# A decay table laid out with its heads innermost and moved on ScalarE's DMA queue

## The chip, the cores and the metric

The kernel runs on one core of a Trainium2 chip. The metric is the device time of one execution in microseconds, smaller is better. TensorE does matmuls, VectorE and ScalarE elementwise work (ScalarE also moves data out of PSUM), GpSimd slow elementwise work and scattered DMAs; in this kernel every ordinary DMA is issued from SyncE's queue.

## The reference

Three layers follow each other: a decayed linear attention (2 batches, 8 heads, 768 positions, head size 64), an MLP with a hard-swish, and a mixture of 8 experts in which each expert takes at most 192 of the 1536 tokens, in the order of their logits.

```python
# attention, per block: Dmask[i,j] = lam**(i-j) for i >= j, else 0
intra = (qb @ kb.T * Dmask) @ vb
inter = (qb * lam_pow) @ kv_state
kv_state = lam_block * kv_state + (kb * rev_pow).T @ vb
...
h = x @ w_in                     # 1536 x 512 @ 512 x 2048
g = h * clip(h + 3, 0, 6) / 6
x2 = g @ w_out                   # 2048 x 512
...
logits = x2 @ w_gate             # greedy assignment, capacity 192
out[mask] = relu(x2[mask] @ w1[e]) @ w2[e]
```

## The kernel before, in words

The 1536 tokens are 12 chunks (c0 to c11) of 128, six for each batch. For a chunk, attention needs its raw data (`raw`, loaded in two halves: q and k for the scores, then v and k), the products of scores and decay mask (`sm`), the keys scaled by decay (`kd`, eight ScalarE steps, one a head), the running state (`sbd`, faded on ScalarE and added to on VectorE), and then `outs` on TensorE (`xo`). The result goes out of PSUM as two f16 parts (`xT`: high part on ScalarE, L504, rest on VectorE, L505).

The MLP's first product (`h`, L221 to L223, three matmuls for each pair of f16 parts) needs `xT` and converted weights. w_in and w_out come as 64-bit floats, in 8 blocks each, and `weights` turns a block into two f16 parts: clear the sign (L381 on VectorE or L383 on ScalarE), a max (L385, VectorE or GpSimd), shift (L387), two merges (L389, L391), then the high part on ScalarE (L406) and the low one on VectorE (L416). After a product, ScalarE and VectorE make g (L535, L536, L406, L416). Then come the logits (L610), seven rounds of token assignment (L800 to L809 on VectorE) with the second product (`x2p`, L647) run beside them, scattering, and the experts (L922, L952).

The order of the work is written by a planner: `add` records a step with an engine, an estimated cost, dependencies, buffers and a key; `run` repeatedly emits the step that by its estimates can start first, with the lower key first among those that start within a small window. The order it writes is fixed in each engine's queue, so an engine waits at a step even if a later one could go. Every load on SyncE is such a step.

All decays come from one small table, `tab`. Each partition holds the powers of four heads (128 zeros, 1, then 128 powers), which VectorE makes by seven doublings (`powers`, L268 to L277). Two DMAs on SyncE's queue write the rows of two partitions to DRAM (`tz`, L306), and a third (L311) reads them back into all partitions with a start that is one element later in each, so that every partition gets its row of the decay mask for 8 heads: 1024 pieces of 512 bytes. These DMAs stand between the loads of the first chunk and the others. `kdec` (L359) and `sm` (L458) wait for the third; `qd` (L443) and the fade (L474) use the powers themselves.

Of the kernel before, what the change touches and what calls it, by code (L numbers as in the profile page):

```python
# [5 lines left out]
F32 = mybir.dt.float32  # L6
# [3 lines left out]
AF = mybir.ActivationFunctionType  # L10
# [38 lines left out]
class Plan:  # L49
# [143 lines left out]
def fused_kernel(ctx, tc, raw_d, lam_d, win_d, wout_d, wg_d, w1_d, w2_d, out):  # L193
# [23 lines left out]
    def C(shape, dt, name):  # L217
        return cst.tile(shape, dt, name=name)
# [4 lines left out]
        te.matmul(ps, ll, rh, start=False, stop=stop)  # L223


    lam = C([P, 4], F32, "lam")
    sy.dma_start(lam, lam_d)
    raws = {}
    plan.clk["ve"] = 0.6
# [31 lines left out]
    tabb = buf("B", [P, 2052], F32, "tab")  # L261
    sbdb = buf("B", [P, 3, 4, 64], F32, "sbd")
    held += [tabb, sbdb]
    for b in held[2:]:
        b.left += 1
    pw, dec = (lambda: tabb.tile[:, 0:1028].rearrange("p (h x) -> p h x", h=4)), None

    def powers():  # L268
        x = pw()
        ve.memset(x[:, :, 0:128], 0.0)  # L270
        ve.memset(x[:, :, 128:129], 1.0)
        ve.tensor_copy(x[:, :, 129], lam)
# [26 lines left out]
    pw = pw()
    tab = tabb.tile  # L300
    sbd = [sbdb.tile[:, i] for i in range(3)]
    dec = tab[:, 1028:2052].rearrange("p (r h i) -> p r h i", r=2, h=4)
    qdec = pw[:, :, 129:257]
# [3 lines left out]
    plan.dma = max(plan.dma, 6.7)
    plan.clk["sp"] = 5.4
    plan.steps = list(parts[1])
    plan.run()  # L310
# [43 lines left out]
    plan.clk.update(ve=5.4, ge=3.4, se=2.0, sp=7.6)  # L354
# [71 lines left out]
    def attention(c, key):  # L426
# [7 lines left out]
        if s < 5:  # L434
            kd = buf("Q", [P, 512], F32, f"kd{c}")

            def kdm():
                for h in range(8):
                    se.activation(kd[:, 64 * h:64 * h + 64], r[:, 3, 64 * h:64 * h + 64], AF.Copy, scale=kdec[:, h:h + 1])  # L439
            t_kd = add("se", 1.6, kdm, ld + [t_kdec], [r, kd], key)  # L440
        if s:
            qd = buf("Q", [P, 4, P], F32, f"qd{c}")
            t_qd.append(add("ve", 0.62, lambda: ve.tensor_tensor(qd[:], r[:, 0].rearrange("p (h i) -> p h i", h=4), qdec, op=OP.mult),  # L443
                            ld[:1], [r, qd, tabb], key))
# [10 lines left out]
        for i in range(2):  # L455
            sm = buf("Q", [P, 4, P], F32, f"sm{c}_{i}")
            sms.append(sm)
            t_mk.append(add("ve", c_ve(512), lambda i=i, sm=sm: ve.tensor_tensor(sm[:], pss[i][:], dec[:, i], op=OP.mult),  # L458
                            [t_ss, dec_in], [pss[i], sm, tabb], key))
        if s < 5:  # L460
            pk = buf("pE" if c > 3 else "pC", [P, 4, 64], F32, f"kv{c}")

            def kv():
                for hp in range(4):
                    for par in range(2):
                        cl = slice(P * hp + 64 * (par ^ hp & 1), P * hp + 64 * (par ^ hp & 1) + 64)
                        te.matmul(pk[64 * par:64 * par + 64, hp], kd[:, cl], r[:, 2, cl], start=True, stop=True)
            t_kv = kv_done[c] = add("pe", 0.66, kv, [t_kd] + ld, [kd, r, pk], key)
# [532 lines left out]
def pack(inputs):  # L1001
# [17 lines left out]
    lam = np.repeat(lam, 64, axis=0)  # L1019
# [22 lines left out]
```

## Time and profile before

| | |
|---|---|
| median of 3 runs | 514.68 us (512.02 to 515.46) |
| profiled execution | 515.91 us, of which span 514.0 us |
| TensorE / VectorE / ScalarE / GpSimd busy | 485.0 / 397.8 / 309.0 / 166.6 us |
| DMA | 77.86 MB, mean 151 GB/s |
| mean granted TensorE clock | 0.986 |

Busy times add up every stage; the kernel has a start, a long MLP stage to about 205 us, the assignment to about 340 us and the experts, each with its own limit. Matmuls overlap in the records, so a busy TensorE can still have room.

### The profile page before, as it was taken

What the parts mean: (1) busy time and instruction counts of PE and PEld (TensorE: products, weight loads), DVE (VectorE), ACT (ScalarE), POOL (GpSimd) and SP (SyncE); (2) the same over time, 40 slices, a digit from 0 to 9 for tenths busy, and PEclk for the clock granted to TensorE, in tenths of its full rate; (3) what the DMA queues carried; (4) which work ended last, traced back from release to release, by engine and by line L of the source; (5) the groups of instructions that cost most, each with busy time, mean ns of one, the idle gap of its engine ahead of it and who ended that gap; (6) DMA issues with size and microseconds to landing.
All of it is one profiled execution on the core that took longest, in us unless ns stands there. A gap on an engine that the chain in (4) does not pass through costs nothing.

```text
span 514.0 us, 10307 instructions
## 1 busy us (share of the span) xinstructions
PE 485.0 (94%) x4241; PEld 296.7 (58%) x4243; DVE 397.8 (77%) x707; ACT 309.0 (60%) x486; POOL 166.6 (32%) x174
## 2 busy tenths in 40 slices
PE   7687998999999999999999999999969999999995
PEld 3476444688785444534434443556459676776762
DVE  7689999988688877589899889877524878889620
ACT  1476959764556664377669558745423767687510
POOL 2013343120222220167347436618860312223211
PEclk9889999999999999999999999999979999999999
DMA  7999326220264550000000000667368999995011
GB/s 224 400 416 412 148 83 246 84 42 2 83 246 91 97 94 8 2 1 1 1 1 2 1 1 7 240 246 240 132 149 261 327 400 356 360 354 215 1 42 41
DMA packets 44910, 77.86 MB, mean 151 GB/s; under 512 B 33080, under 2 KB 34112, under 8 KB 38720
## 3 DMA queue, kind: packets, MB, share of 16 engines
q1 hardware_dynamic: 42752, 70.82, 41.0%
q0 software_dynamic: 2112, 6.39, 3.3%
q8 instruction: 33, 0.54, 0.4%
q14 instruction: 13, 0.11, 0.1%
HBM read 63.46 MB, written 6.40 MB: 136 GB/s over the span
## 4 chain that ended last, share of the span: by engine, by line
DVE 38%; issue 22%; PE 18%; POOL 8%; ACT 8%; DMA 5%; POOLq 0%; SPq 0%; DVEq 0%; ACTq 0%
PE x2p L647 9%; DVE G L809 7%; DVE r L536 4%; DVE G L800 3%; DVE g L416 3%; POOL w L410 3%; POOL out L877 2%; ACT kd L439 2%; DVE sm L458 2%; ACT g L406 2%; DVE eq L782 2%; PE h L221 2%; DVE wid L391 2%; PE cp L828 2%; PE h L223 2%
## 5 line engine op out<-in xcount | busy, mean ns | idle before, releaser
L647 PE MATMUL x2p<-wo,g 128*128 128x512 f16 (+1 forms) x576 | 124.6, 362 | 0.0
L221 PE MATMUL h<-xT,wi 128*128 128x256 f16 (+2 forms) x304 | 90.8, 306 | 2.8 <-DVE r L536 2.8
L222 PE MATMUL h<-xT,wi 128*128 128x256 f16 (+2 forms) x304 | 90.7, 306 | 0.0
L223 PE MATMUL h<-xT,wi 128*128 128x256 f16 (+2 forms) x304 | 90.6, 306 | 0.0
L647 PEld LDWEIGHTS <-g 128*128 128x128 f16 x576 | 52.5, 99 | 55.6 <-issue 10.5
L775 POOL TENSOR_SCALAR eq<-mrow,m 128x128 bf16<-128x128 f32 x56 | 56.7, 1030 | 84.6 <-DVE on L748 52.1
L416 DVE SCALAR_TENSOR_TENSOR w<-ws,w 128x1024 f16<-128x1024 f32 x58 | 71.4, 1276 | 5.8 <-ACT w L406 5.8
L922 PE MATMUL hp<-xs,w 128*128 128x192 f16 x768 | 67.4, 251 | 3.8 <-DMA xs<-xsa 3.8
L922 PEld LDWEIGHTS <-w 128*128 128x128 f16 x768 | 65.1, 100 | 7.6 <-issue 5.2
L952 PE MATMUL po<-w,h 128*64 128x512 f16 (+1 forms) x384 | 64.1, 380 | 0.1
L406 ACT ACTIVATE w<-ws 128x1024 f16<-128x1024 f32 x64 | 63.9, 1048 | 0.1
L809 DVE TENSOR_SCALAR G<-mrow,m 128x1408 bf16<-128x1408 f32 (+10 forms) x77 | 52.0, 706 | 0.0
L385 POOL TENSOR_SCALAR wod<-wod 128x1024 f32<-128x1024 f32 x8 | 22.5, 2818 | 89.3 <-ACT wod L383 75.5
L406 ACT ACTIVATE g<-r 128x512 f16<-128x512 f32 (+1 forms) x52 | 30.8, 595 | 30.5 <-DVE r L536 29.6
L952 PEld LDWEIGHTS <-h 128*64 128x64 f16 (+1 forms) x384 | 29.0, 104 | 31.8 <-issue 1.7
L416 DVE SCALAR_TENSOR_TENSOR g<-r,g 128x512 f16<-128x512 f32 (+1 forms) x52 | 34.3, 662 | 11.4 <-ACT g L406 11.0
L536 DVE SCALAR_TENSOR_TENSOR r<-r,h 128x512 f32<-128x512 f32 (+1 forms) x52 | 33.1, 639 | 10.1 <-ACT r L535 9.8
L535 ACT ACTIVATE r<-h,c 128x512 f32<-128x512 f32 (+1 forms) x52 | 33.4, 644 | 10.9 <-PE h L223 10.8
L803 ACT ACTIVATE G<-mrow,m 128x1536 bf16<-128x1536 f32 (+3 forms) x28 | 39.4, 1407 | 0.8
L222 PEld LDWEIGHTS <-wi 128*128 128x128 f16 x304 | 30.6, 101 | 15.9 <-issue 3.2
L928 ACT ACTIVATE rr<-hp 128x384 f32<-128x384 f32 x32 | 15.6, 490 | 40.0 <-PE hp L922 39.8
L221 PEld LDWEIGHTS <-wi 128*128 128x128 f16 x304 | 30.5, 100 | 15.0 <-issue 1.5
(154 smaller groups left out, 693.2 us busy)
## 6 DMA issues: line engine op xcount, KB each, us to landing
ws<-w SPq DMA_DIRECT2D x32, 1024.0 KB, 9.3
raw<-raw SPq DMA_DIRECT2D x24, 512.0 KB, 10.0
wis<-w_in SPq DMA_DIRECT2D x8, 1024.0 KB, 14.1
wos<-w_out SPq DMA_DIRECT2D x8, 1024.0 KB, 7.8
tab<-tz SPq DMA_DIRECT2D x1, 512.0 KB, 6.3
wt<-wo SPq DMA_TRANSPOSE x16, 3.2
xsa<-xa,pos POOLq DMA_INDIRECT x12, 4.9
xsb<-xb,pos POOLq DMA_INDIRECT x12, 2.7
```

Source lines behind the costliest of these rows:

```text
L221: te.matmul(ps, lh, rh, start=start, stop=False)
L222: te.matmul(ps, lh, rl, start=False, stop=False)
L223: te.matmul(ps, ll, rh, start=False, stop=stop)
L406: h = add("se", c_se(n), lambda: se.activation(dst()[0], src(), AF.Copy, scale=sc), deps, bufs, key, reserve)
L416: lo = add("ve", c_ve(n), lambda: ve.scalar_tensor_tensor(dst()[1], src(), sc, dst()[0], op0=OP.mult, op1=OP.subtract), [h], bufs, key)
L536: t = add("ve", c_ve(nf * T), lambda: ve.scalar_tensor_tensor(r[:], r[:], 6.0 * 2.0 ** -11, ps[:], op0=OP.min, op1=OP.mult), [t], [ps, r], ...
L647: te.matmul(ps[:], gsl(y, fc, j), w[:, z, fc % 4, d0:d1], start=(fc + y + z == 0), stop=(fc == 15 and y == 1))
L775: t_eq.append(add("ge", 1.06, lambda i=i, eq=eqs[0], mrow=mrow: ge.tensor_scalar(eq[:, i], mrow[:, P * i:P * i + P], m[:, i:i + 1], None, ...
L803: se.activation(G[:, z, 0:o], mrow[:, 0:o], AF.Sign, scale=-1.0, bias=m[:, i:i + 1])
L809: ve.tensor_scalar(G[:, z, o:], mrow[:, o:], m[:, i:i + 1], None, op0=OP.is_le)
L922: te.matmul(ps[:, i], w[:, z, kk % 2, cl], x[:, 2 * kk + y, CAP * i0:CAP * i0 + CAP], start=(i + kk + y + z == 0), stop=(i == 1 and kk == ...
L952: te.matmul(o, h1[e][:, y, k, cl], w2[e, fh][0][:, zz, f], start=(k + y + zz == 0), stop=(k == 7 and y == 1))
```

## The change

- **Table.** `xp` holds, in every partition, the powers of all 8 heads with the head as the innermost index (256 x 8). One DMA of 8 KB on ScalarE's queue writes one partition of it to DRAM, a second one on the same queue reads it back with a start 8 elements later in each partition: 128 pieces of 4 KB. ScalarE then turns the order from (position, head) into (head, position) (`dec_in`, one step of 1024 columns), and makes the powers of the own heads (`own`, two steps of 512 columns on 64 partitions) for `qd` and the fade. SyncE's queue holds loads alone, in the order w0, q0, q1, v0, v1.
- **kd.** The eight scalings of a chunk become two planner steps of four, with a key that is 2 higher, so that `xT` of the same chunk goes ahead of them.
- **Conversion.** Blocks 1 and 2 of w_in clear the sign on ScalarE (L383) and take the max on GpSimd (L385), as blocks 3 to 7 do; block 0 stays on VectorE.

```diff
-    lam = C([P, 4], F32, "lam")
+    lam = C([P, 8], F32, "lam")
...
+    xpb = buf("B", [P, 256, 8], F32, "xp")
+    tabb = buf("B", [P, 512 + 1024], F32, "tab")
+    sbdb = buf("B", [P, 768 + 1024], F32, "sbd")
...
     def powers():
-        x = pw()
-        ve.memset(x[:, :, 0:128], 0.0)
-        ve.memset(x[:, :, 128:129], 1.0)
-        ve.tensor_copy(x[:, :, 129], lam)
+        x = xpb
+        ve.memset(x[:, 0:127], 0.0)
+        ve.memset(x[:, 127:128], 1.0)
+        ve.tensor_copy(x[:, 128], lam)
         n = 1
         while n < 128:
-            ve.tensor_tensor(x[:, :, 129 + n:129 + 2 * n], x[:, :, 129:129 + n],
-                             x[:, :, 128 + n:129 + n].to_broadcast([P, 4, n]), op=OP.mult)
+            ve.tensor_tensor(x[:, 128 + n:128 + 2 * n], x[:, 128:128 + n],
+                             x[:, 127 + n:128 + n].to_broadcast([P, n, 8]), op=OP.mult)
             n *= 2
...
-    tz = dram.tile([2, 4, 256], F32, name="tz")
-    for par in range(2):
-        sy.dma_start(tz[par:par + 1], pw[64 * par:64 * par + 1, :, 0:256])
...
-    sy.dma_start(dec, bass.AP(tensor=tz.tensor, offset=tz.offset + 1, ap=[[1, P], [256, 8], [1, P]]))
...
+    tz = dram.tile([256 * 8], F32, name="tz")
+    se.dma_start(tz[:].rearrange("(o n) -> o n", o=1), xpb.tile[0:1].rearrange("p n c -> p (n c)"))
+    se.dma_start(decs, bass.AP(tensor=tz.tensor, offset=tz.offset, ap=[[8, P], [1, 1024]]))
...
+    dec_dma = Step({}, [], [], 0, 0, 0)
+    dec_dma.end, dec_dma.on = 9.6, "dma"
...
+    def own():
+        for par in range(2):
+            pr = slice(64 * par, 64 * par + 64)
+            se.activation(qdec[pr], xpb[pr, 128:256, 4 * par:4 * par + 4].rearrange("p i h -> p h i"), AF.Copy)
+    t_own = add("se", 1.2, own, (), [xpb, tabb], 1)
+    dec_in = add("se", 1.1, lambda: se.activation(dec.rearrange("p r h i -> p (r h) i"), decs.rearrange("p (i c) -> p c i", c=8), AF.Copy),
+                 [dec_dma], [tabb, sbdb, xpb], -1)
...
-            early = by_cols and k < 3
+            early = by_cols and k < 1
...
-            def kdm():
-                for h in range(8):
+            def kdm(z):
+                for h in range(4 * z, 4 * z + 4):
                     se.activation(kd[:, 64 * h:64 * h + 64], r[:, 3, 64 * h:64 * h + 64], AF.Copy, scale=kdec[:, h:h + 1])
-            t_kd = add("se", 1.6, kdm, ld + [t_kdec], [r, kd], key)
+            t_kd = [add("se", 0.96, lambda z=z: kdm(z), ld + [t_kdec], [r, kd], key + 2) for z in range(2)]
...
-                        se.activation(sb[:, hp], old[:, hp], AF.Copy, scale=pw[:, hp, 256:257])
+                        se.activation(sb[:, hp], old[:, hp], AF.Copy, scale=qdec[:, hp, 127:128])
```

## Rows read from the trace of the kernel before

**Rows 1.** Busy time by stretch: engines, TensorE's granted clock, DMA share, GB/s

```profile
0.00:20.00 20.00, 12.58 (x81) 6.21 (x82) 13.37 (x35) 6.41 (x19) 2.65 (x18) 1.00 0.83 281
20.00:40.00 20.00, 17.13 (x256) 14.74 (x256) 16.78 (x28) 13.59 (x46) 2.81 (x1) 0.83 1.02 415
60.00:80.00 20.00, 19.05 (x142) 9.49 (x140) 19.86 (x28) 13.61 (x32) 5.83 (x2) 1.00 0.24 82
80.00:100.00 20.00, 18.67 (x176) 11.20 (x176) 19.97 (x34) 16.07 (x42) 5.91 (x2) 1.00 0.49 183
...
98.00:355.00 257.00, 253.64 (x2166) 141.15 (x2164) 215.43 (x439) 160.89 (x211) 90.93 (x83) 1.00 0.22 64
```

**Rows 2.** The chain that ended last, pieces in order: start us, us, what

```profile
6.01 1.72 DMA tz<-tab
8.25 7.60 DMA raw<-raw
15.93 3.93 ACT kd L439 x16
...
28.15 1.91 ACT kd L439 x8
...
345.17 9.77 PE x2p L647 x60
```

**Rows 3.** Timeline, 0 to 31 us: start us, us, engine, line, operation [idle before <-releaser]

```profile
2.48 0.85 DVE L272 COPY tab<-lam 128x4 f32<-128x4 f32 x1 [0.61 <-DMA lam<-lam]
...
7.81 0.39 SPq L311 DMA_DIRECT2D tab<-tz  x1
...
14.12 0.38 DVE L359 COPY kdec<-tab 128x2 f32<-128x2 f32 x4 [2.51 <-DMA tab<-tz]
14.40 2.48 DVE L458 TENSOR_TENSOR sm<-S,tab 128x512 f32<-128x512 f32 x4
...
15.98 1.09 PE L498 MATMUL xo<-sm,raw 128*64 128x128 f32 x16 [2.45 <-DMA raw<-raw]
...
19.77 0.63 ACT L504 ACTIVATE xT<-xo 128x256 f16<-128x256 f32 x2
20.16 0.75 DVE L505 SCALAR_TENSOR_TENSOR xT<-xo,xT 128x256 f16<-128x256 f32 x2 [2.15 <-ACT xT L504]
...
21.98 0.29 PE L221 MATMUL h<-xT,wi 128*128 128x128 f16 x1
...
25.79 0.45 PE L494 MATMUL xo<-qd,sbd 64*64 64x128 f32 x8
...
30.36 0.76 DVE L505 SCALAR_TENSOR_TENSOR xT<-xo,xT 128x256 f16<-128x256 f32 x2 [1.12 <-ACT xT L504]
```

**Rows 4.** The instructions on tile tab: ns min/median/max, first and last start us

```profile
L275 DVE TENSOR_TENSOR tab<-tab x7: 166/191/424, 3.4 to 4.8; 128x4 f32<-128x4 f32 x1, 128x8 f32<-128x8 f32 x1, 128x16 f32<-128x16 f32 x1, 128x32 f32<-128x32 f32 x1
```

**Rows 5.** Busy time by stretch of 1 us; the last two columns are DMA share and GB/s

```profile
10.00:11.00 1.00, 0.90 (x16) 0.90 (x16) 1.00 (x2) 0.00 (x0) 0.00 (x0) 1.00 1.03 207
...
16.00:17.00 1.00, 1.00 (x16) 0.83 (x16) 1.00 (x3) 1.00 (x5) 0.00 (x0) 1.00 1.00 414
```

**Rows 6.** GpSimd's output scatters (L877): in 400 to 445 us, then 445 to 514 us

```profile
DMA to landing us min/median/max: 6.1/8.1/8.3
...
DMA to landing us min/median/max: 2.7/2.7/8.2
```

**Rows 7.** The instructions on tile wid: ns min/median/max, first and last start us

```profile
L387 DVE TENSOR_SCALAR wid<-wid x8: 678/684/1400, 7.8 to 77.0; 128x1024 int32<-128x1024 int32 x8
...
L383 ACT ACTIVATE wid<-wis x5: 1140/1151/1160, 35.3 to 67.7; 128x1024 f32<-128x1024 f32 x5
L385 POOL TENSOR_SCALAR wid<-wid x5: 2766/3067/3492, 36.5 to 68.9; 128x1024 f32<-128x1024 f32 x5
L381 DVE TENSOR_SCALAR wid<-wis x3: 682/684/699, 6.4 to 35.9; 128x1024 int32<-128x1024 int32 x3
L385 DVE TENSOR_SCALAR wid<-wid x3: 677/681/695, 7.1 to 37.8; 128x1024 f32<-128x1024 f32 x3
```

More of the change, by code (lines that the diff above doesn't have):

```diff
@@ L259, in load_w @@
             deps, [st], key, 3, 1 << 20)
-    tabb = buf("B", [P, 2052], F32, "tab")
-    sbdb = buf("B", [P, 3, 4, 64], F32, "sbd")
-    held += [tabb, sbdb]
+    xpb = buf("B", [P, 256, 8], F32, "xp")
+    tabb = buf("B", [P, 512 + 1024], F32, "tab")
+    sbdb = buf("B", [P, 768 + 1024], F32, "sbd")
+    held += [tabb, sbdb, xpb]
     for b in held[2:]:
         b.left += 1
-    pw, dec = (lambda: tabb.tile[:, 0:1028].rearrange("p (h x) -> p h x", h=4)), None
     def powers():
-        x = pw()
-        ve.memset(x[:, :, 0:128], 0.0)
-        ve.memset(x[:, :, 128:129], 1.0)
-        ve.tensor_copy(x[:, :, 129], lam)
+        x = xpb
+        ve.memset(x[:, 0:127], 0.0)
+        ve.memset(x[:, 127:128], 1.0)
+        ve.tensor_copy(x[:, 128], lam)
         n = 1
         while n < 128:
-            ve.tensor_tensor(x[:, :, 129 + n:129 + 2 * n], x[:, :, 129:129 + n],
-                             x[:, :, 128 + n:129 + n].to_broadcast([P, 4, n]), op=OP.mult)
+            ve.tensor_tensor(x[:, 128 + n:128 + 2 * n], x[:, 128:128 + n],
+                             x[:, 127 + n:128 + n].to_broadcast([P, n, 8]), op=OP.mult)
             n *= 2
-    FIRST = [["w0", "q0"], ["q1"], ["v0", "v1"]]
     ld_raw, win_ld, first = {}, {}, {}
-    for i, nm in enumerate(sum(FIRST, [])):
+    for i, nm in enumerate(["w0", "q0", "q1", "v0", "v1"]):
         c = int(nm[1])
@@ L288, in fused_kernel @@
             first["q%d" % c], first["v%d" % c] = ld_raw[c]
-    for i, nm in enumerate(sum(FIRST, [])):
+    for i, nm in enumerate(["w0", "q0", "q1", "v0", "v1"]):
         first[nm].key, first[nm].reserve = i - 9, 0
-    add("ve", 3.9, powers, (), [tabb])
-    add("ge", 0.1, lambda: ge.memset(sbdb[:, 0], 0.0), (), [sbdb])
+    add("ve", 4.4, powers, (), [xpb])
+    add("ge", 0.1, lambda: ge.memset(sbdb[:, 0:256], 0.0), (), [sbdb])
+    add("ge", 0.1, lambda: ge.memset(tabb[:, 0:1], 0.0), (), [tabb])
     held += [raws[c] for c in ld_raw] + [x[0] for x in win_ld.values()]
-    for b in held[4:]:
+    for b in held[5:]:
         b.left += 1
-    parts = [[first[n] for n in p] for p in FIRST]
-    plan.steps = [x for x in plan.steps if x not in parts[1] + parts[2]]
     plan.run()
[L299 to L303, printed above, removed]
-    tz = dram.tile([2, 4, 256], F32, name="tz")
-    for par in range(2):
-        sy.dma_start(tz[par:par + 1], pw[64 * par:64 * par + 1, :, 0:256])
[L307 to L310, printed above, removed]
-    sy.dma_start(dec, bass.AP(tensor=tz.tensor, offset=tz.offset + 1, ap=[[1, P], [256, 8], [1, P]]))
-    plan.dma = max(plan.dma, 8.8) + 1.46
-    plan.steps = parts[2] + [late_warm]
+    qdec = tabb.tile[:, 0:512].rearrange("p (h i) -> p h i", h=4)
+    decs = tabb.tile[:, 512:1536]
+    sbd = [sbdb.tile[:, 256 * i:256 * i + 256].rearrange("p (h d) -> p h d", h=4) for i in range(3)]
+    dec = sbdb.tile[:, 768:1792].rearrange("p (r h i) -> p r h i", r=2, h=4)
+    tz = dram.tile([256 * 8], F32, name="tz")
+    se.dma_start(tz[:].rearrange("(o n) -> o n", o=1), xpb.tile[0:1].rearrange("p n c -> p (n c)"))
+    se.dma_start(decs, bass.AP(tensor=tz.tensor, offset=tz.offset, ap=[[8, P], [1, 1024]]))
+    plan.dma = max(plan.dma, 8.0) + 1.46
+    plan.steps = [late_warm]
     kdec = C([P, 8], F32, "kdec")
@@ L353, in fused_kernel @@
     ve.tensor_copy(sel8f, sel8)
-    plan.clk.update(ve=5.4, ge=3.4, se=2.0, sp=7.6)
+    plan.clk.update(ve=6.3, ge=3.4, se=6.5, sp=3.5)
     def make_kdec():
@@ L359, in make_kdec @@
                 ve.tensor_copy(kdec.rearrange("p (h r) -> p r h", r=2)[:, par, z::2], dec[:, par ^ z, z::2, P - 1])
-    dec_in = Step({}, [], [], 0, 0, 0)
-    dec_in.end, dec_in.on = plan.dma + 0.9, "dma"
-    t_kdec = add("ve", 0.4, make_kdec, [dec_in], [tabb], 0)
+    dec_dma = Step({}, [], [], 0, 0, 0)
[7 more added lines that the diff above has]
+                 [dec_dma], [tabb, sbdb, xpb], -1)
+    t_kdec = add("ve", 0.4, make_kdec, [dec_in], [sbdb], 0)
+    xpb.left -= 1
+    held.remove(xpb)
     def weights(src, store, scale, nm, key, lo_eng, ldkey, after=None, gate=lambda k: (), pre={}):
@@ L443, in attention @@
             t_qd.append(add("ve", 0.62, lambda: ve.tensor_tensor(qd[:], r[:, 0].rearrange("p (h i) -> p h i", h=4), qdec, op=OP.mult),
[L444 removed]
+                            ld[:1] + [t_own], [r, qd, tabb], key))
         pss = [buf("pA" if c == 1 else "pB", [P, 4, P], F32, f"S{c}_{i}") for i in range(2)]
@@ L458, in attention @@
             t_mk.append(add("ve", c_ve(512), lambda i=i, sm=sm: ve.tensor_tensor(sm[:], pss[i][:], dec[:, i], op=OP.mult),
-                            [t_ss, dec_in], [pss[i], sm, tabb], key))
+                            [t_ss, dec_in], [pss[i], sm, sbdb], key))
         if s < 5:
@@ L467, in kv @@
                         te.matmul(pk[64 * par:64 * par + 64, hp], kd[:, cl], r[:, 2, cl], start=True, stop=True)
-            t_kv = kv_done[c] = add("pe", 0.66, kv, [t_kd] + ld, [kd, r, pk], key)
+            t_kv = kv_done[c] = add("pe", 0.66, kv, t_kd + ld, [kd, r, pk], key)
             sb, old = sbd[c % 3], sbd[(c + 2) % 3]
@@ L1018, in pack @@
     lam[:, 1::2] = lam[::-1, 1::2].copy()
-    lam = np.repeat(lam, 64, axis=0)
+    lam = np.repeat(lam.reshape(1, 8), P, axis=0)
     wi = np.asarray(inputs["moe_w_in"]).reshape(4, P, 8, 256).transpose(2, 1, 0, 3)
```

## Prediction

> **What bounds the kernel now.** I read the busy time by stretch first, then the chain of waits, then the timeline of the first 36 us. From 98 to 355 us TensorE is busy 253.64 of 257 us [rows 1], and the chain ends that stage on TensorE itself, with 9.77 us of x2p and nothing else to wait for [rows 2]: whatever TensorE hasn't done by 98 us comes out at the end. From 60 to 100 us VectorE is busy 39.83 of 40 us and TensorE 37.72 [rows 1], so there VectorE sets the pace. Before that neither is full: VectorE lacks 6.63 us in the first 20 and 3.22 in the next 20 [rows 1]. Nothing behind 355 us is touched. So the change is worth what it takes off VectorE's idle and busy time ahead of about 98 us, as far as TensorE can follow.
>
> The start is a chain: table out, table back (asked for at 7.81, there when kdec starts at 14.12: 6.3 us) [rows 3], v and k of the first chunk (7.60 us from issue, landing at 15.85) and then 3.93 us of kd of two chunks on ScalarE [rows 2], behind which xT of the first chunk stands until 19.77 although its xo was done at 17.07; the first h comes at 21.98 [rows 3]. 10 us later the same happens with one chunk: kd, 1.91 us [rows 2], ahead of an xT for which VectorE waits 1.12 us [rows 3].
>
> **The table's way out.** VectorE's seven doublings work on 508 elements a partition now and on 1016 after; by the shortest and the longest of them an element costs (424 - 166) / 252 = 1.02 ns [rows 4], so +0.52 us and an end at 5.2 + 0.5 = 5.7 us. The zeros double too (about +0.5 us), in the 0.61 us in which VectorE waits for lam [rows 3]: no delay, but busy time. Then one write instead of two. Now it lands 1.72 us after its issue [rows 2]. After, SyncE's queue never stops for the table, so the engines are busy with loads when the write comes. No row shows two such queues at once; the nearest is GpSimd's scatter, 2.7 us mostly alone and 8.1 us beside a full load queue [rows 6], 5.4 us more. So 1.7 to 7.1 us; I take 2.7, because the write is a single row and the engines were already partly busy when it took 1.72. It lands at 5.75 + 2.7 = 8.45 us.
>
> **The table's way back.** 512 KB in 1024 pieces moved at 207 GB/s with full engines, where loads in large pieces move 414 [rows 5]; in 4 KB pieces it should move like a load, 1.25 us alone, 2.5 us if it shares the engines half and half. With 1.7 us from issue to landing: 4.2 us. Ends: 2.9 us, unshared, and 8.1 us as the loaded scatter [rows 6]. It lands at D = 8.5 + 4.2 = 12.7 us, with ends of 5.75 + 1.7 + 2.9 = 10.4 and 5.75 + 7.1 + 8.1 = 21.0.
> By the round-robin between queues that the Trainium skill states (DMA: Bandwidth & Descriptors, "Queues, rings and completion order"), an engine turns to the other queue after a packet, so neither transfer stands behind the whole backlog; that is the half and half above, and the ends at 21.0 would then not be reached. The loaded scatter, at three times its time alone, neither proves nor refutes it.
>
> **From D to the first h.** ScalarE's reordering: 1.15 us, from a 1024-column step with a strided input (L383) [rows 7]; 0.05 for the handover; kdec 0.28; two products, half of 2.48, so 1.24; 0.08; xo 1.09; xT on both engines 1.14 (19.77 to 20.91); two handovers 0.09 [rows 3]. Sum 5.12 us, so h at 17.8 instead of 21.98: 4.2 us earlier. It needs v0, which by then isn't late: 3.1 MB of first loads and the table's 0.5 at 414 GB/s [rows 5] from 2.5 us on (when lam, the first load, is in [rows 3]) are done at 11.2. Almost all of the 4.2 us is kd's place in the queue; the table itself comes 1.4 us earlier and loses 1.2 in the reordering.
>
> **kd behind xo.** The same eight scalings, so no work is saved. Behind them wait kv, the state and the next chunk's xo: kd of c0 would end near 19.5 and the state near 20.7, before the 25.8 at which xo of c1 ran [rows 3]. If that cover goes, the next chunk pays up to 1.9 us.
>
> **New waits.** ScalarE stands at the second DMA until the write has landed and at the reordering until D. Behind it stand `own` (needed by qd of c1, 0.7 us of VectorE work with slack) and the high part of w_in's block 0, from which VectorE makes 1.2 us of low part, also needed by h. Products and low part then share VectorE between 14 and 18 us: 0 to 0.3 us. On SyncE three issues and their waits go; the loads behind them come up to 4 us sooner. They were not what VectorE waited for after 20 us, so I count nothing.
>
> **Two blocks shared out.** VectorE loses 2 x (0.684 + 0.681) = 2.73 us. ScalarE gets 2 x 1.15 us, GpSimd 2 x 3.07 us [rows 7], where it is empty (2.65 of 20 us [rows 1]). But a VectorE step beside a GpSimd max gets longer: L387 took 1.40 us once instead of 0.68 [rows 7], and I take 0.72 us for each max, between 0 and all of 3.07. Net -1.3 us.
>
> **The sum.** VectorE's idle time to 40 us is 9.85 us. After: 1.0 at the start and before lam; from 12.1 (it was free at 11.6 [rows 3], +0.5) to kdec at 13.9, 1.8; 0.5 for the first xT instead of 2.15; 0.4 of small ones; and half of the 3.22 us in 20 to 40 us, since the wait of 1.12 us goes and others, such as for TensorE, stay: 1.6. That is 5.3, so 4.55 us less idle. Add 1.0 us of new table work and take off 1.3: -4.85 us. TensorE can follow: it starts 4.2 us sooner and has 2.87 + 0.95 + 1.33 us of idle in the stretches of 20 to 40 and 60 to 100 us [rows 1]; from 98 us on it carries the gain to the end unchanged. The profiled execution, 515.91 us, would become 511.1; the median of the runs is 1.2 us (0.2%) lower, so 514.68 - 4.9 = 509.8 us.
>
> **The rivals.**
> A, more than that: D at 10.4 (2.3 us sooner), all idle in 20 to 40 us gone (1.6 more): -8.8, 505.9 us. For it: the granted clock was 0.83 on average in that stretch [rows 1], partly at 1.2 and partly at 2.4 GHz, TensorE having waited for xT before, and an unbroken start would give that back. Against: VectorE has no work ready before D.
> B, the waits close up again: after the first chunk the planner's order meets other waits, idle in 20 to 40 us stays 3.22 and the moved blocks gain nothing: 4.85 - 1.6 - 1.3 = 1.9 us, 512.8 us. For it: the order was written for estimates (the table at 9.6 us) that the chip misses by some 3 us.
> C, slower: the table stands behind the loads. It decides at D = 21.98 - 5.12 = 16.9; at D = 21.0 the first h comes 4.1 us late, less perhaps 1 us of conversion that VectorE finds to do: +3.1, 517.8 us. For it: the loaded scatter. Against: the table is issued after only some 4 us of loads were moved, and half of any wait falls on a write of one row.
> D, GpSimd's max stops VectorE for as long as it runs: 6.14 us instead of 1.44, so -4.85 + 4.7 = -0.15, 514.5 us. Against: the longest L387 lost 0.72 us.
> That is the exclusive lock of the port pair that VectorE and GpSimd share, as the Trainium skill has it (SBUF — State Buffer, "Who interferes with whom"): the loser is fully blocked. The lengthened L387 agrees in kind; how long the block lasts depends on which of the two began.
>
> **How the numbers follow.** Forecast 0.46, A 0.18, B 0.19, C 0.10, D 0.07. The forecast's own spread is about 1.5 us either way, from D and the half of 3.22. A measurement can tell about 1% of this kernel, 5.15 us, and the forecast lies just inside: a bit under half of its chance is below 509.5. Faster 0.20 + 0.18 = 0.38 and a little for a larger effect, 0.40; slower by over 1% needs more than C's price, 0.06; same 0.54. The range runs from A to just above D's 514.5, leaving out C: 505.7 to 515.5 us.
>
> **What would show it.** Right: the write and the read on ScalarE's queue landing near 8.5 and 12.7 us; the first xT directly behind its xo; first h near 18; VectorE idle by 40 us near 5.3 us; the stage of x2p ending about 5 us before 355. Wrong: a table that lands after 17 us (C), VectorE steps of 2 to 3 us beside GpSimd's max (D), or a first h at 18 and yet the same time at 98 us (B).

## The result, and the profile after

The changed kernel takes 520.27 us (median of 4 runs, 519.16 to 520.70), against 514.64 us for the kernel before (4 runs, 512.02 to 515.46): 1.0106 of the time, 95% interval 1.0078 to 1.0134. It is 5.6 us slower where 4.9 us were forecast as a gain, and it lies above the range. The profiled execution took 520.20 us, 4.3 more than that of before; its span is 518.5 us.

In the profile after, all lines behind L362 are 2 higher (L504 is L506); in the experiments they shift by their own edits. First the page's part on DMA issues (KB each, median us from issue to landing), the one row of the table's way back:

```profile
tab<-tz ACTq DMA_DIRECT2D x1, 512.0 KB, 7.5
```

It was forecast at 4.2 us. The timeline of the first 30 us, which answers to [rows 3] (start us, us, engine, line, operation, [idle before <-releaser]):

```profile
1.70 2.14 SPq L249 DMA_DIRECT2D raw<-raw  x4
...
3.88 0.46 SPq L257 DMA_DIRECT2D wis<-w_in  x1
...
4.39 7.13 SPq L249 DMA_DIRECT2D raw<-raw  x4
...
5.79 0.48 ACTq L302 DMA_DIRECT2D tz<-xp  x1
...
11.87 0.35 ACTq L303 DMA_DIRECT2D tab<-tz  x1
12.25 1.28 ACT L358 ACT_TABLE_LOAD   x1 [12.25 <-DMA tz<-xp]
...
13.55 2.27 ACT L358 ACTIVATE tab<-xp 64x512 f32<-64x512 f32 x2
...
15.84 0.69 DVE L445 TENSOR_TENSOR qd<-raw,tab 128x512 f32<-128x512 f32 x1 [6.79 <-ACT tab L358]
...
19.35 2.04 ACT L360 ACTIVATE sbd<-tab 128x1024 f32<-128x1024 f32 x1 [3.54 <-DMA tab<-tz]
...
21.42 0.38 DVE L351 COPY kdec<-sbd 128x2 f32<-128x2 f32 x4 [2.49 <-ACT sbd L360]
...
22.24 2.96 ACT L441 ACTIVATE kd<-raw,kdec 128x64 f32<-128x64 f32 x12
...
22.45 2.56 PE L500 MATMUL xo<-sm,raw 128*64 128x128 f32 x16 [5.93 <-DVE sm L460]
...
25.11 0.62 ACT L506 ACTIVATE xT<-xo 128x256 f16<-128x256 f32 x2
...
26.76 1.02 PE L469 MATMUL kv<-raw,kd 128*64 128x64 f32 x16
...
28.80 0.69 PE L469 MATMUL kv<-raw,kd 128*64 128x64 f32 x16
...
29.42 0.23 PE L221 MATMUL h<-xT,wi 128*128 128x128 f16 x1
```

The powers end where the forecast has them, and the write goes out at 5.79. But ScalarE's queue asks for the read only at 11.87: the 8 KB took 6.1 us instead of 2.7. The table is there at 19.35, not at 12.7, and the first h starts at 29.42 instead of 21.98 [rows 3]. When the write goes out, SyncE has issued two blocks of w_in (1 MB each, the first at 1.24 us) and five half chunks (0.5 MB each; of the last line's four only the first, the next follows at 8.27): 4.7 MB, of which the engines have moved 1.2 (204 GB/s over 5.79 us). So 3.5 MB of loads stand ahead of the write.

The stretches, answering to [rows 1] and, for two short ones, to [rows 5] (busy time of TensorE, its weight loads, VectorE, ScalarE and GpSimd; granted clock; DMA share; GB/s):

```profile
0.00:20.00 20.00, 13.23 (x61) 5.97 (x62) 10.44 (x26) 4.19 (x4) 2.68 (x19) 0.91 0.88 333
20.00:40.00 20.00, 15.84 (x228) 12.16 (x228) 16.04 (x31) 19.16 (x58) 5.72 (x3) 0.83 1.02 417
...
98.00:355.00 257.00, 253.64 (x2179) 141.12 (x2178) 214.65 (x441) 160.73 (x214) 85.85 (x73) 1.00 0.21 60
...
16.00:18.00 2.00, 0.52 (x3) 0.02 (x1) 1.97 (x3) 0.00 (x0) 0.00 (x0) 1.00 1.04 422
...
22.00:24.00 2.00, 1.55 (x12) 1.25 (x14) 2.00 (x4) 2.00 (x9) 0.00 (x0) 0.50 0.99 414
```

VectorE's idle time to 40 us has grown from 9.85 to (20 - 10.44) + (20 - 16.04) = 13.5 us; it was to fall to 5.3. While the table's read is under way the DMA engines are full, at 422 GB/s; during the write they moved 345 GB/s. From 98 to 355 us TensorE is as busy as before, to the hundredth: 253.64 us.

The end of the kernel can be read from three tiles. `pos` holds the positions that the assignment gives the tokens. The rows of x2 (`xa` its first 384 columns, `xb` the rest) are scattered to DRAM in the order of the experts (`xsa`, `xsb`) and read back transposed (`xs`); `hp` and `po` are an expert's first and second product. First after (instruction, count, shortest/median/longest ns, first and last start in us), then before:

```profile
L649 PE MATMUL x2p<-wo,g x576: 322/379/391, 181.7 to 365.6; 128*128 128x512 f16 x128, 128*128 128x384 f16 x64
...
L867 DVE CAST pos<-vm x1: 173/173/173, 353.7 to 353.7; 128x12 int32<-128x12 f32 x1
...
L924 PE MATMUL hp<-xs,w x768: 242/247/365, 383.3 to 496.6; 128*128 128x192 f16 x192
```

```profile
L647 PE MATMUL x2p<-wo,g x576: 322/379/390, 205.0 to 362.4; 128*128 128x512 f16 x128, 128*128 128x384 f16 x64
...
L865 DVE CAST pos<-vm x1: 173/173/173, 346.1 to 346.1; 128x12 int32<-128x12 f32 x1
...
L922 PE MATMUL hp<-xs,w x768: 246/246/364, 378.3 to 492.2; 128*128 128x192 f16 x192
```

The last x2p starts 3.2 us later than before (362.4), the positions that end the assignment are known 7.6 us later (before 346.1), and the first expert product, hp, starts 5.0 us later (378.3). From there to the last product of all the time is 128.9 us against 129.4. So the loss is made of two terms: **3.2 us until x2p ends, and 1.8 us between that and the first hp** (17.7 instead of 15.9 us). With the 0.5 us gained behind it that is 4.5 us, as much as the spans differ.

The second term is seen in the timeline at the last of the twelve xsa scatters, first of after, then of before:

```profile
369.05 0.80 SPq L977 DMA_DIRECT2D ws<-w  x2
...
372.06 1.96 POOL L879 DMA_INDIRECT xsa<-xa,pos  x1 [0.19 <-DVE w L418]
...
378.09 5.55 SPq L899 DMA_TRANSPOSE xs<-xsa  x2
```

```profile
368.86 1.97 POOL L877 DMA_INDIRECT xsa<-xa,pos  x1 [0.19 <-DVE w L416]
...
372.47 5.84 SPq L897 DMA_TRANSPOSE xs<-xsa  x2
```

The scatter starts 6.5 us after the last x2p in both, but SyncE could go on to the transposes 6.0 us later after the change and 3.6 us later before. The stretches beside that scatter, the first of after, the second of before, show what differs:

```profile
372.00:374.00 2.00, 2.00 (x11) 0.92 (x10) 2.00 (x3) 0.12 (x1) 1.94 (x1) 1.00 1.01 426
...
370.00:372.00 2.00, 2.00 (x11) 0.88 (x9) 1.13 (x1) 0.00 (x0) 1.81 (x3) 1.00 0.26 98
```

After, two expert weights of 1 MB each (ws) were issued at 369.05 and fill the DMA engines while the scatter's data are under way. Before, the two issues next ahead of the scatter were at 351.3 and 353.6 us, and the engines moved 98 GB/s beside it. Run 7 below has the same instructions as after without those loads there.

### The profile page after: what moved, and what is told of

Read it like the earlier page. It is cut to its first block, busy times and chain, and to the rows that moved or that the text cites. A ratio compares the mean times of both kernels' runs of the same rounds, so it can differ in the third digit from the quotient of the medians.

```text
span 518.5 us, 10330 instructions
## 1 busy us (share of the span) xinstructions
PE 486.3 (94%) x4241; PEld 295.4 (57%) x4243; DVE 400.7 (77%) x703; ACT 315.4 (61%) x491; POOL 174.3 (34%) x177
## 4 chain that ended last, share of the span: by engine, by line
PE 45%; DVE 29%; issue 9%; DMA 7%; ACT 5%; POOL 4%; POOLq 0%; DVEq 0%; ACTq 0%
PE x2p L649 10%; PE hp L924 7%; DVE G L811 7%; PE po L954 6%; PE h L221 5%; PE h L223 5%; PE h L222 5%; DVE G L802 3%; DMA ws<-w 3%; POOL xsb L879 2%; DVE g L418 2%; DVE r L538 2%; PE xo L500 2%; DVE eq L784 2%; PE cp L830 2%
## 5 line engine op out<-in xcount | busy, mean ns | idle before, releaser
L221 PE MATMUL h<-xT,wi 128*128 128x256 f16 (+2 forms) x304 | 88.5, 301 | 2.7 <-DVE r L538 1.2
L223 PE MATMUL h<-xT,wi 128*128 128x256 f16 (+2 forms) x304 | 88.4, 301 | 0.4 <-DVE wi L418 0.4
L222 PE MATMUL h<-xT,wi 128*128 128x256 f16 (+2 forms) x304 | 88.4, 301 | 0.0
L387 POOL TENSOR_SCALAR wod<-wod 128x1024 f32<-128x1024 f32 x8 | 24.1, 3008 | 102.0 <-ACT wod L385 102.0
L418 DVE SCALAR_TENSOR_TENSOR g<-r,g 128x512 f16<-128x512 f32 (+1 forms) x52 | 35.6, 695 | 7.0 <-ACT g L408 6.4
L222 PEld LDWEIGHTS <-wi 128*128 128x128 f16 x304 | 29.7, 98 | 16.0 <-issue 2.7
L223 PEld LDWEIGHTS <-wi 128*128 128x128 f16 x304 | 29.7, 98 | 15.2 <-DVE wi L418 0.5
L879 POOL DMA_INDIRECT out<-os,rows x12 | 14.2, 1186 | 71.6 <-ACT os L938 71.4
```

Source lines behind the costliest of these rows:

```text
L221: te.matmul(ps, lh, rh, start=start, stop=False)
L222: te.matmul(ps, lh, rl, start=False, stop=False)
L418: lo = add("ve", c_ve(n), lambda: ve.scalar_tensor_tensor(dst()[1], src(), sc, dst()[0], op0=OP.mult, op1=OP.subtract), [h], bufs, key)
```

## The experiments

Twelve kernels ran. Milestones in us from the profiled executions (first start of h, pos, last start of x2p, the gap from there to the first hp, last start of po), read from the views of these tiles; time and ratio from the runs. A profile is one execution: that of before took 1.3 us more than the median of its runs, so differences of a microsecond between two rows' milestones say little.

| kernel | time, ratio [95%] | h | pos | x2p | gap | po |
|---|---|---|---|---|---|---|
| before | 514.64 | 22.0 | 346.1 | 362.4 | 15.9 | 507.7 |
| changed | 520.27, 1.0106 [1.0078, 1.0134] | 29.4 | 353.7 | 365.6 | 17.7 | 512.2 |
| 1 kd alone | 519.34, 1.0105 [1.0068, 1.0142] | 20.8 | 345.5 | 361.0 | 21.4 | 511.0 |
| 2 conversion alone | 519.25, 1.0099 [1.0064, 1.0133] | 22.2 | 353.5 | 362.0 | 17.7 | 511.1 |
| 3 changed, table on SyncE | 515.00, 1.0019 [0.9996, 1.0041] | 21.2 | 347.6 | 359.5 | 17.7 | 506.7 |
| 4 changed, own first | 520.02, 1.0109 [1.0074, 1.0144] | 28.7 | 353.0 | 365.0 | 17.7 | 512.2 |
| 5 before, order | 516.30, 1.0041 [1.0021, 1.0060] | 22.2 | 352.0 | 363.1 | 17.0 | 509.9 |
| 6 kd alone, order | 512.37, 0.9978 [0.9957, 0.9998] | 20.1 | 342.6 | 359.5 | 15.3 | 503.6 |
| 7 changed, order | 517.16, 1.0046 [1.0027, 1.0065] | 29.3 | 348.8 | 365.3 | 15.4 | 510.2 |
| 8 changed, loads held | 515.67, 1.0026 [1.0006, 1.0047] | 21.9 | 348.3 | 360.2 | 17.5 | 507.0 |
| 9 as 3, order | 513.37, 0.9985 [0.9970, 1.0001] | 22.5 | 345.0 | 361.5 | 15.5 | 506.3 |
| 10 kd and conversion, order | 513.65, 0.9981 [0.9964, 0.9998] | 20.3 | 343.9 | 360.4 | 15.3 | 505.6 |
| 11 before, other order | 514.95, 1.0016 [0.9996, 1.0036] | 21.8 | 342.4 | 362.2 | 15.5 | 506.4 |
| 12 kd and conversion | 514.93, 1.0012 [0.9996, 1.0029] | 20.7 | 348.1 | 360.0 | 17.5 | 507.5 |

Ratios are to runs of the kernel before on the same chip (medians 514.09 for 1 to 4, 513.99 for 5 to 8, 514.31 for 9 to 12). One theory was that the late table costs everything (T1), the other that the order of the later work, which the planner writes anew after any edit, costs as much (T2).

**1. Kd in halves alone** (before, with the two hunks on kd of the change).

> The kernel before with kd in halves behind xT as the only change. If the late table (11.9 us for the write's landing, 19.35 us for the mask) made the change slow and kd's place was worth what I priced, the first xT follows its xo at 17.1 us, the first h starts near 18 instead of 22 us, and the time falls by 2 to 4 us, to 511 to 513. If the loss came from the new order of ScalarE's work (ScalarE busy 19.2 of 20 us between 20 and 40 us in the changed kernel), this part already shows it: 516 or more.

519.34 us, slower by 5.3, although x2p ends 1.4 us earlier than before. The timeline of this kernel shows where it went:

```profile
367.37 0.55 DVE L662 SCALAR_TENSOR_TENSOR xa<-x2p,xa 128x384 f16<-128x384 f32 x1
...
373.98 0.96 POOL L877 DMA_INDIRECT xsa<-xa,pos  x1 [0.19 <-issue]
```

The low part of the last xa stands behind four steps of expert weights on VectorE, and the last xsa scatter behind eight xsb scatters on GpSimd: it runs 13.0 us after the last x2p, where it ran 6.5 us after it before. The first h came at 20.8 us, not near 18. An edit of ScalarE's steps in the first 100 us seems to cost 5 us at 370 us through the order; run 6 tests that.

**2. Conversion alone.**

```diff
-            early = by_cols and k < 3
+            early = by_cols and k < 1
```

> The kernel before with blocks 1 and 2 of w_in shared out (sign on ScalarE, max on GpSimd) as the only change. Late table as the cause: no loss here, 513 to 515. Sharing out as the cause (longer latency of a block over three engines, VectorE held up beside GpSimd, a later order in which the logits come 14 us later): 517 to 520.

519.25 us. The tiles of w_out's low part and of pos:

```profile
L416 DVE SCALAR_TENSOR_TENSOR wo<-wod,wo x8: 1219/1226/1227, 99.7 to 204.1; 128x1024 f16<-128x1024 f32 x8
...
L865 DVE CAST pos<-vm x1: 174/174/174, 353.5 to 353.5; 128x12 int32<-128x12 f32 x1
```

The last w_out block is converted at 204.1 us instead of 189.3, so the gate product and the logits come late and pos 7.4 us late. Two blocks of w_in moved off VectorE at 20 to 40 us, and the planner put w_out's blocks later. The time is the one that was expected if the sharing out is the cause; that it is the order it brings, and not its work, is shown by run 12, where the same edit beside kd costs nothing.

**3. The changed kernel with the table's DMAs on SyncE's queue**, between the loads as before (the planner's time for SyncE is set back with them, so it writes another order too).

```diff
+    parts = [[first["q1"]], [first["v0"], first["v1"]]]
+    plan.steps = [x for x in plan.steps if x not in parts[0] + parts[1]]
...
-    se.dma_start(tz[:].rearrange("(o n) -> o n", o=1), xpb.tile[0:1].rearrange("p n c -> p (n c)"))
-    se.dma_start(decs, bass.AP(tensor=tz.tensor, offset=tz.offset, ap=[[8, P], [1, 1024]]))
+    sy.dma_start(tz[:].rearrange("(o n) -> o n", o=1), xpb.tile[0:1].rearrange("p n c -> p (n c)"))
+    plan.dma = max(plan.dma, 6.7)
+    plan.clk["sp"] = 5.4
+    plan.steps = list(parts[0])
+    plan.run()
+    sy.dma_start(decs, bass.AP(tensor=tz.tensor, offset=tz.offset, ap=[[8, P], [1, 1024]]))
...
-    plan.steps = [late_warm]
+    plan.steps = parts[1] + [late_warm]
...
-    plan.clk.update(ve=6.3, ge=3.4, se=6.5, sp=3.5)
+    plan.clk.update(ve=6.3, ge=3.4, se=6.5, sp=7.6)
```

> The changed kernel with its new table, but both table DMAs on SyncE's queue and between the loads, where they stood in the kernel before. Late table as the cause: the write lands within 2 us (near 7.6 us), the mask near 12 to 13 us, the reordered mask is ready by 15, the first h comes near 20 instead of 29.4 us, and the time falls to 509 to 513. If the order of the later work is the cause, the first h comes early and the time stays at 517 or more. If 4 KB pieces are no faster, the mask still lands after 14 us.

515.00 us: 5.3 us of the loss are gone (4.5 by the ratios), 2 us short of the 509 to 513 expected. Its timeline:

```profile
7.63 0.33 SPq L309 DMA_DIRECT2D tab<-tz  x1
...
13.28 2.04 ACT L366 ACTIVATE sbd<-tab 128x1024 f32<-128x1024 f32 x1 [3.84 <-DMA tab<-tz]
...
16.18 2.96 ACT L447 ACTIVATE kd<-raw,kdec 128x64 f32<-128x64 f32 x12
...
19.04 0.63 ACT L512 ACTIVATE xT<-xo 128x256 f16<-128x256 f32 x2
...
21.20 0.23 PE L221 MATMUL h<-xT,wi 128*128 128x128 f16 x1
```

The write lands within 1.84 us and the table is there at 13.28, close to the 12.7 that was forecast for it. Yet the first h comes at 21.20, not at 17.8. The 4 KB pieces need 13.28 - 7.63 = 5.65 us where the small ones needed 6.3 [rows 3]. That is not a gain of the pieces that can be counted on: in run 9 the large ones took 6.2 us in the same place (7.75 to 13.98), and the small ones took 5.0 in run 6 (8.02 to 13.02) and 6.9 in run 2 (7.82 to 14.75).

**4. The own powers ahead of the read** on ScalarE's queue.

```diff
     se.dma_start(tz[:].rearrange("(o n) -> o n", o=1), xpb.tile[0:1].rearrange("p n c -> p (n c)"))
+    own()
     se.dma_start(decs, bass.AP(tensor=tz.tensor, offset=tz.offset, ap=[[8, P], [1, 1024]]))
...
-    t_own = add("se", 1.2, own, (), [xpb, tabb], 1)
+    t_own = Step({}, [], [], 0, 0, 0)
+    t_own.end, t_own.on = 9.4, "se"
```

> The changed kernel with the two steps that make the own powers put ahead of the second table DMA on ScalarE, so that they no longer stand behind the landing of the write. Late table as the cause: VectorE's stop of 6.8 us at the first qd goes and the two merges of block 0 run at 9 to 12 us, but the mask still lands after 18 us, so the first h moves by 0 to 2 us and the time stays at 518 to 520. If the stop of VectorE at qd is the cause, the first h comes 4 us or more earlier and the time is 514 to 516.

520.02 us. VectorE's stop of 6.79 us at qd is gone, in the timeline:

```profile
10.23 0.68 DVE L447 TENSOR_TENSOR qd<-raw,tab 128x512 f32<-128x512 f32 x1
...
19.39 2.04 ACT L362 ACTIVATE sbd<-tab 128x1024 f32<-128x1024 f32 x1 [9.47 <-DMA tab<-tz]
```

and the time is the same, because the table lands at 19.39 as it did without the edit; h and x2p come only 0.7 and 0.6 us earlier. That stop was a wait in the shadow of another.

**5. The kernel before in another order**: the same instructions, the w_out conversions with a key 8 higher.

```diff
-    w0_key = unit_key[4, 0] - 16
+    w0_key = unit_key[4, 0] - 16 + 8
```

> The kernel before with the keys of the w_out conversions 8 higher: the same instructions and data, only another order written by the planner. Theory now: part of every change's effect is the order of the later work (kd alone and sharing out alone each cost 5 us although they started earlier). Then this too moves the time by 3 to 6 us, to 517 to 520, with the same first h at 22 us and later logits or scatters. Rival, that kd and the sharing out cost by themselves: the time stays at 513 to 515.5.

516.30 us: pos comes 5.9 us later and the time is 2.3 us longer with nothing else changed. That is less than the 3 to 6 us expected and more than the rival's range, with an interval clear of 1: T2 is real for the kernel before as well.

**6. Kd in halves, w_out with a key 4 lower.** Run 1, and `- 16 - 4` in the line above.

> The kernel before with kd in halves, as in the run of kd alone, and the keys of the w_out conversions 4 lower. Order as the cause of its 5.2 us: the first h stays near 21 us, the last scatter of xsa comes right after the last x2p and the time falls to 510 to 514. kd itself as the cause: it stays at 518 to 520.

512.37 us, 7.0 less than run 1 (6.5 by the ratios) with the same instructions, and the only version besides run 10 whose interval lies below 1. Its timeline also shows what became of kd's place:

```profile
15.45 2.97 ACT L439 ACTIVATE kd<-raw,kdec 128x64 f32<-128x64 f32 x12 [3.16 <-DMA raw<-raw]
15.50 1.09 PE L498 MATMUL xo<-sm,raw 128*64 128x128 f32 x16 [2.02 <-DMA raw<-raw]
...
18.33 0.63 ACT L504 ACTIVATE xT<-xo 128x256 f16<-128x256 f32 x2
...
20.14 0.23 PE L221 MATMUL h<-xT,wi 128*128 128x128 f16 x1
```

xo is done at 16.6, but xT starts at 18.33: twelve of the sixteen scalings still stand ahead of it.

**7. The changed kernel, w_out with a key 8 lower.**

> The changed kernel with the keys of the w_out conversions 8 lower. The table still lands at 19 us and the first h comes at 29 us. If the late table by itself costs 5 us and the order adds the rest, the time falls a little, to 516 to 519. If the order is the whole loss, it falls to 512 to 515. If order plays no part: 520.

517.16 us, 3.1 less than the changed kernel with the same instructions and the same late table. The gap is 15.4 us. Timeline and stretch, to be held against those of after above:

```profile
371.78 1.97 POOL L879 DMA_INDIRECT xsa<-xa,pos  x1 [0.19 <-DVE w L418]
...
375.41 2.60 SPq L899 DMA_TRANSPOSE xs<-xsa  x1
```

```profile
372.00:374.00 2.00, 2.00 (x11) 0.94 (x10) 2.00 (x2) 0.00 (x0) 1.87 (x2) 1.00 0.10 37
```

Here the DMA engines are nearly idle beside the last scatter (37 GB/s instead of 426) and SyncE goes on after 3.6 us instead of 6.0.

**8. The changed kernel with its loads held.** Both table transfers stay on ScalarE's queue; SyncE reads 32 bytes of `tz` ahead of q1, so that it issues no more loads until the write has landed; the split into `parts` and the planner's time for SyncE are those of run 3.

```diff
     se.dma_start(tz[:].rearrange("(o n) -> o n", o=1), xpb.tile[0:1].rearrange("p n c -> p (n c)"))
+    hold = C([1, 8], F32, "hold")
+    sy.dma_start(hold, tz[0:8].rearrange("(o n) -> o n", o=1))
+    plan.dma = max(plan.dma, 6.7)
+    plan.clk["sp"] = 5.4
+    plan.steps = list(parts[0])
+    plan.run()
     se.dma_start(decs, bass.AP(tensor=tz.tensor, offset=tz.offset, ap=[[8, P], [1, 1024]]))
```

> The changed kernel with both table DMAs on ScalarE's queue, but SyncE reads 32 bytes of the written table ahead of its load of q1, so that q1 and all later loads wait until the write has landed. Loads in the way as the cause of the late table: the write lands within 2.5 us instead of 6, the mask by 14 to 16 us, the first h near 22 and the time at 514 to 516, as with the table on SyncE's queue. ScalarE's queue itself as the cause: the write takes 5 us or more again, and the time stays at 519 to 521.

515.67 us. Its timeline:

```profile
5.79 0.48 ACTq L304 DMA_DIRECT2D tz<-xp  x1
...
7.66 0.35 ACTq L311 DMA_DIRECT2D tab<-tz  x1
...
11.66 2.04 ACT L368 ACTIVATE sbd<-tab 128x1024 f32<-128x1024 f32 x1
...
14.07 0.69 DVE L453 TENSOR_TENSOR qd<-raw,tab 128x512 f32<-128x512 f32 x1 [3.75 <-DMA raw<-raw]
```

The write takes 1.87 us and the read 4.0. So ScalarE's queue is as quick as SyncE's; what made both transfers late was the loads on SyncE's queue, and those issued ahead of them above all. Here SyncE had issued 1.6 MB when the write went out, of which 1.1 were moved (190 GB/s over 5.79 us): 0.5 MB stood ahead of it instead of 3.5. The hold ends with the write. From 8.01 us on SyncE issues loads again, and yet the read, asked for at 7.66, was not held up as in the changed kernel: of the 0.8 MB that the engines moved in its 4.0 us (198 GB/s) the table was two thirds.

The hold has its price. The loads come later: VectorE stands at the first qd for q1 until 14.07, and kdec behind it runs at 15.81 although the mask was in order at 13.70. The first h comes at 21.9 us, no earlier than in the kernel before.

**9. Run 3 with w_out's key 8 lower.**

> The changed kernel with its two table transfers on SyncE's queue between the loads (measured before: 515.0 us, ratio 1.0019), and all w_out conversions with a key 8 lower, so that the same instructions come in another order. If the order of the later work eats the early gain, the logits' product comes at about 201 to 203 us instead of 206.6 and the time falls by 2 to 4 us: 511 to 513 us. If order plays no part, it stays at 515.0 us, within 1 us.

513.37 us, 1.6 less than run 3 and 0.4 above the upper end expected if order plays a part, with the logits at 203.4 us: the gap falls from 17.7 to 15.5 us, and x2p ends 2.0 us later, so that little of it is left.

**10. Kd and conversion with the old table, w_out's key 8 lower.**

> The kernel before with its old table, kd in halves and the sharing out of two blocks, and the w_out conversions with a key 8 lower. Against the run above it has another table and the same rest: if the new layout with 4 KB pieces gains nothing once it isn't late (its read 0.7 us faster, its reordering 2.04 us longer), this one is equal or up to 1.5 us faster, 510.5 to 513 us; if the new layout is worth what the forecast said (1.4 us sooner in spite of the reordering), it is 1 to 2 us slower, 513 to 515 us. Against the version with kd in halves and a better order alone (512.37 us) it says what the sharing out is worth: 511 us if it takes off 1.3 us, 512.4 us or more if nothing.

513.65 us. The number lies in the range for a layout that is worth what was forecast, but it is only 0.3 us above run 9, and by the ratios (0.9981 and 0.9985) there is nothing between them; nor between this run and run 6 (0.9978). The intervals leave about 1.2 us open either way, and each kernel has an order of its own. So far as these runs can tell, neither the new layout nor the sharing out is worth anything.

**11. The kernel before, w_out's key 4 higher.**

> The kernel before, with the same instructions and the w_out conversions with a key 4 higher. It asks whether an order alone gives what kd in halves with a better order gave (512.37 us). If the gain there was order alone, 512 to 513 us; if it needs the earlier start of the first chunks, 514 to 516 us, no better than before.

514.95 us, no gain: pos comes 3.7 us earlier and the gap is 0.4 us shorter, but x2p ends where it did. Run 6's gain needs its earlier x2p.

**12. Kd and conversion, old table, keys as they were.**

> The kernel before with kd in halves and the sharing out, both at once, old table and no change of keys: the change without its table. With the table on SyncE's queue (515.0 us) it differs in the layout of the table alone. If the new layout is worth nothing by itself, 514 to 516 us; if the parts simply add up from their single runs (+5.3 and +5.2 us), 525 us; if the order decides, anything between 512 and 520 us, told by when the logits' product comes and by the last scatters ahead of the first expert.

514.93 us. The parts do not add up: 5.3 and 5.2 us alone are 0.3 us together. It is the change without its table, so the table part costs 520.27 - 514.93 = 5.3 us (4.8 by the ratios); and run 3, the same with a new table in time, is equal to it.

**What follows from all.** The time is mostly ruled by x2p's end and the gap: from the first hp to the last po it is 128.6 to 130.0 us in every kernel but run 2, where it is 131.4. There TensorE waits 2.77 us inside hp, at 394.4, for the transpose of xsb, which SyncE starts at 391.4 us instead of 383.2 before. Of the runs with pos at least 16 us ahead of the last x2p (before, 6, 7, 9, 10, 11), all have a gap of 15.3 to 15.9 us; of those with 8 to 12 us (after, 2, 3, 4, 5, 8, 12), all have 17.0 to 17.7. Run 1, at 15.5 us, had 21.4 by its order of scatters. T1 accounts for x2p: 360.0 us without the new table (run 12), 365.6 with it. T2 accounts for the gap (run 7 has the late table and a gap of 15.4 us), and for what is lost of an early x2p.

## Why the prediction was wrong, step by step

**"I take 2.7" for the write, and "half and half" for the read: this is the step that failed.** The two measured 6.1 and 7.5 us, so that D was 19.35 instead of 12.7. That is rival C, which was given 0.10, near its own end of 21.0. But its price was too small as well: with its 5.12 us from D to h, D = 19.35 would give a first h at 24.5, and it came at 29.4. The bounds held (1.7 to 7.1, 2.9 to 8.1) and the choice within them was wrong: I put the loaded scatter [rows 6] aside because the write is one row and only some 4 us of loads had been moved, and the loaded scatter was the nearest row after all. What had been moved was the wrong thing to count, as run 8 bears out: 3.5 MB had been issued and not moved, since SyncE no longer stops for the table. While the write was under way the engines moved 2.1 MB (345 GB/s over 6.08 us), more than half of that. In the 7.5 us of the read they moved about 7.5 x 0.42 = 3.1 MB, of which the table was 0.5: a sixth, not half. Run 8 shows the cause, not only the coincidence: with the loads ahead of the write held back the same transfers on the same queue took 1.87 and 4.0 us, and the time fell by 4.6 us (4.1 by the ratios).

"In 4 KB pieces it should move like a load" was not seen either: in run 3, with the read under way, the engines moved 193 GB/s from 11 to 12 us and 201 from 12 to 13, at shares of 0.99 and 0.84, no more than the 207 of the small pieces [rows 5]. Why is open.

The Trainium skill's round-robin (DMA: Bandwidth & Descriptors, "Queues, rings and completion order"), by which 21.0 was not to be reached, was read as if it gave each queue half of the engines. The rows here don't show the order of packets, so they neither confirm nor refute the rule; they refute the half.

**"From D to the first h", 5.12 us: too short by 2.8 us even with a table in time.** In run 3 it is 21.20 - 13.28 = 7.92 us. The reordering took 2.04 us instead of 1.15 (0.9 more). Sixteen xo matmuls, one chunk's, took 2.57 us instead of 1.09: TensorE had stood idle for 2.92 us before them, and the granted clock was 0.75 in 16 to 18 us and 0.50, which is 1.2 GHz, in 18 to 20. From the start of sm to the end of xo 3.31 us instead of 2.41 (0.9 more). And warm-up matmuls (`wb`, until 20.65) and kv, 0.69 us, stand ahead of h in TensorE's order, so that h starts 1.0 us after xT's end (0.9 more). VectorE's idle time to 40 us is 8.1 us in run 3, not the 5.3 of the sum. In the changed kernel itself 10.07 us: there warm-up matmuls, kv twice and a set of scores stand ahead of h, 3.2 us from the end of xT (26.25) to 29.42.

**"Almost all of the 4.2 us is kd's place": failed in size.** With the old table the time from kdec to h fell from 21.98 - 14.12 = 7.86 us [rows 3] to 20.8 - 14.7 = 6.1 in run 1: 1.8 us. Halves with a later key moved four of the sixteen scalings behind xT; twelve went on ahead of it (run 6's timeline shows the same), for the planner emits what can start by its estimates. I had taken the words of the change for the order that it would write.

**"Own" and the new waits: mis-sized, but free.** Own took 2.27 us instead of the 1.2 of its planner step, behind a table load of 1.28 that itself stood behind the write's wait, and qd held up VectorE for 6.79 us with block 0's merges behind it. I had called that slack. Run 4 shows that it cost nothing that can be measured beside D.

**The sharing out, "net -1.3 us": not seen.** GpSimd's max did not stop VectorE for long, so rival D falls. The tile `wid` of after, which answers to [rows 7]:

```profile
L389 DVE TENSOR_SCALAR wid<-wid x8: 681/686/1207, 8.4 to 80.1; 128x1024 int32<-128x1024 int32 x8
...
L393 DVE SCALAR_TENSOR_TENSOR wid<-wis,wid x8: 1224/1225/2014, 17.7 to 82.7; 128x1024 int32<-128x1024 int32 x8
```

The longest took 0.52 and 0.79 us more than the median, near the 0.72 taken, and none 2 to 3 us more. But the work that was freed did not come out at the end: run 10 is level with run 6. Its visible effect is run 2's order, w_out's conversion 14.8 us later.

**"From 98 us on it carries the gain to the end unchanged": failed, on its own.** TensorE is full there in every run, as the forecast said (253.3 to 253.7 us of 257 in the changed kernel and in runs 3, 6, 10 and 11), but an earlier x2p is not an earlier end. Run 3 ends x2p 2.9 us before the kernel before and gains nothing. "Nothing behind 355 us is touched" was true of the instructions and false of their order. That is rival B's thought, the planner's order meeting other waits, in a place where I had not looked: at the assignment's end and the scatters, not in 20 to 40 us. What it costs by itself is 1.8 us of after's loss, 2.3 us in run 5 and 7.0 us (6.5 by the ratios) between runs 1 and 6.

Put together: kd and sharing out end x2p 2.4 us sooner (run 12) and lengthen the gap by 1.6; the late table puts x2p's end back by 5.6. Against run 12 the first h is 8.7 us late (29.4 and 20.7) and the end of x2p 5.6; where the 3.1 us between were absorbed was not measured. What stays open too: in what order the DMA engines took the pieces of the two queues. The write landed when 2.1 MB had been moved since its issue, so it did not wait for all of the 3.5 MB ahead of it; no row shows more. Runs 3, 8 and 9 were planned anew with their loads, so a part of their 5 us may be order; that run 3 and run 12 agree within 0.1 us (0.4 by the ratios) speaks against a large one.

## What to carry to other kernels

A small transfer that others wait for does not become prompt by getting a queue of its own: with 3.5 MB of loads issued ahead of it on the other queue it took 6.1 us, with 0.5 MB 1.9. So count what has been issued when it goes out, not what has been moved. What helped was to hold the loads, or to put the transfer between them, and both make the loads later. Where a planner writes the order, cost an edit in the order that it writes, and try several orders of the same instructions before an edit is judged: here they moved the time by up to 7 us, more than the edit itself was worth. And follow a gain to the very end, through the last hand-over between engines, before it is counted.

## What the runs showed of the hardware

- A ScalarE copy of 1024 f32 columns read at a stride of 8 elements took 2.04 us, and one of 512 columns on 64 partitions read the same way 2.27 / 2 = 1.13 us; the step with a stride of 2 that I had priced it by takes 1.15 us for 1024 [rows 7]. By these, a stride of 8 costs 1.8 to 2.0 times as much a column. The Trainium skill has a rule for it that I had not weighed (SBUF — State Buffer, "Door 1: The DMA port swizzle (why `[64,N]` ≈ `[32,N]`)"): an access that goes to a new 16-byte line each time pays, which 32 bytes do and 8 bytes do every other time. The two steps agree with it in kind.
- A first ScalarE operation brought an ACT_TABLE_LOAD of 1.28 us with it, which stands in the engine's order: behind the wait of a DMA issue at 12.25 us, and at 5.84 us where it waited for VectorE's powers alone (run 3).
- The table's read of 512 KB took 5.0 to 6.9 us in pieces of 512 bytes (runs 6 and 2) and 5.65 and 6.2 us in pieces of 4 KB (runs 3 and 9), all on SyncE's queue between the loads: no difference shows. Less issued ahead of it on the other queue shortened it from 7.5 to 4.0 us (after and run 8).
